# A gated linear recurrence and a SwiGLU block on one core: weights narrowed by integer operations on three engines, and another order of loads

## The chip, the cores and the metric

The kernel runs on one core of one Trainium2 chip. The metric is the device time of one execution in microseconds (us). The core has five engines with a queue of instructions each: TensorE (PE, with its weight loads shown as PEld), VectorE (DVE), ScalarE (ACT), GpSimd (POOL) and SyncE (SP), which here issues nearly all DMAs. An engine takes its instructions in program order; a wait in front of one holds all that stand behind it in the same queue.

## The reference, cut to what matters

```python
def _attn_ref(q, k, v, a_re, a_im):            # (4, 8, 768, 48) each
    mag = np.sqrt(a_re * a_re + a_im * a_im)
    scale = np.minimum(mag, 0.999) / (mag + 1e-06)
    a_re_n, a_im_n = (a_re * scale, a_im * scale)
    for t in range(S):
        new_re = ar * S_re - ai * S_im
        new_im = ar * S_im + ai * S_re
        kv = np.einsum('bhd,bhe->bhde', k[:, :, t], v[:, :, t])
        S_re, S_im = (new_re + kv, new_im)
        y[:, :, t] = np.einsum('bhd,bhde->bhe', q[:, :, t], S_re)

def _moe_ref(x, w_gate, w_val, w_out, rms_g):  # x: (3072, 384), d_ff 1536
    rms = np.sqrt(np.mean(x * x, axis=-1, keepdims=True) + 1e-06)
    xn = x / rms * rms_g
    g = xn @ w_gate
    silu = g * (1.0 / (1.0 + np.exp(-g)))
    val = xn @ w_val
    return (silu * val @ w_out).astype(np.float32)
```

The output of the first is laid out as 3072 rows of 384 and goes into the second. The three weight matrices arrive as float64, all other inputs as float32; the kernel computes in float32.

## The kernel before

The time axis is cut into 24 chunks of 128 steps (`C`), and two chunks make a unit (`UC`), so there are 12 units. A batch has three units. Within a chunk the recurrence is written as attention: k and q are turned by the running phase and scaled by the running magnitude of the gates, and a state of 96 x 48 per head carries from chunk to chunk. The work of the fast path (`fast`) lies in lanes, each a generator of steps:

- `load_gates` fetches a unit's gates `re` and `im` (L646, three DMAs each), `load_rows` its `k`, `q` (L662) and `v` (L669).
- `gates` (L683) works out phase and magnitude: about 13 ACT and 20 DVE operations on 128 x 768, in a chain that goes back and forth between the two, and ends with four products `ks`, `k`, `qs`, `q` (L768). `BEHIND` (L681) holds the first ACT step of units 2, 3 and 4 back until weight piece 9, 15 and 17.
- `move_rows` sends the four products to another partition layout, `kr` and `qr`, by three DMAs each (L782), then the decays of the chunks through DRAM and back (`dec` L792, `decay` L795). The second wait there is for a DMA that SP itself issued just before.
- `fetch` loads the float64 weights as pairs of 32-bit words in 18 pieces of 768 KB (L827), and `narrow` (L833) makes float32 of each: a piece has 128 x 768 numbers with a low and a high word. ACT squares the high word read as a float (L847); DVE masks out small values by that square (`masked`), shifts and joins the bits (L861 and the operation behind it), takes the power of two (L867), scales the low word by it and adds. Pieces 0 to 11 are `wg` and `wv` in turn, 12 to 17 are `wo`.
- `scores` runs s_ps = kr'qr (L888), the mask `am` on DVE (L893) and the transposes kt_ps (L907) with their copies `kt` on ACT (L911); `finish` runs state_ps (L928) and y_ps (L950, L953); `normalise` does the RMS norm with `rs` on POOL (L979) and the transposes xT_ps (L995, L1000).
- `feed_forward`, one lane for even and one for odd units, runs per unit 12 tiles gv_ps (L1023; 12 matmuls of 128 x 256 each), silu on ACT (L1027), `hT` on DVE (L587), then out_ps in halves (L1047), which need the `wo` pieces, a copy on ACT (L1056) and the store (L1059). gv_ps has three PSUM buffers.

The order of all instructions is fixed when the program is built. The class `Order` (L45) plays the lanes against each other: every step carries an engine, a planned duration and the names of the steps it waits for; of the steps at the heads of the lanes, the one that could begin first by this plan is written out next. On the chip an instruction waits only for the data and buffers it uses, but it stands in its engine's queue where the plan put it.

At the end a flag `bad` is worked out from range checks (`ok`, L1082). If it is set, a second, general program (`general`) runs after the fast one. With these inputs it isn't set.

Of the kernel before, what the change touches and what calls it, by code (L numbers as in the profile page):

```python
# [20 lines left out]
FP32 = mybir.dt.float32  # L21
I32 = mybir.dt.int32
U32 = mybir.dt.uint32
AF = mybir.ActivationFunctionType
ALU = mybir.AluOpType
# [3 lines left out]
P = 128  # L29
# [10 lines left out]
RE_MIN = 2.0 ** -7  # L40
RE_MAX = 2.0 ** 7
P_MIN = 2.0 ** -40


class Order:  # L45
# [72 lines left out]
def step(engine, us, needs, emit, **more):  # L118
    return engine, us, needs, emit, more
# [429 lines left out]
def fast(tc, ctx, qT, kT, v, a_re, a_im, w_gate, w_val, w_out, rms_g, out, H, bad):  # L549

    nc = tc.nc
    B, DM, S = a_re.shape
# [4 lines left out]
    DF = w_gate.shape[1]  # L557
    ND = DM // P
    NF = DF // P
    UC = 2  # L560
    T = UC * C
    NU = N // UC
# [11 lines left out]
    stage = ctx.enter_context(tc.tile_pool(name="stage", bufs=2))  # L574
    EARLY = 4
# [4 lines left out]
    order = Order()  # L580
    tt_us = lambda n: 0.07 + n / 960
    ts_us = lambda n: 0.07 + n / 1920
    ac_us = lambda n: 0.19 + n / 1200
    pe_us = lambda n: max(0.11, 0.003 + n / 1200)

    def tt(o, x, y, op=ALU.mult):
        nc.vector.tensor_tensor(out=o, in0=x, in1=y, op=op)  # L587

    def stt(o, x, c, y, op0, op1=ALU.mult, **kw):
        nc.vector.scalar_tensor_tensor(out=o, in0=x, scalar=c, in1=y, op0=op0, op1=op1, **kw)  # L590
# [32 lines left out]
    order.clock["POOL"] = 5.0  # L623
    ends = consts.tile([P, NU, ND, UC], FP32, name="ends")
    range_ = consts.tile([P, NU], FP32, name="range_")
    FW = 2 * P
    NW = DF // FW
    wg = consts.tile([P, NW, ND, FW], FP32, name="wg")
    wv = consts.tile([P, NW, ND, FW], FP32, name="wv")
    wo = consts.tile([P, NF, DM], FP32, name="wo")  # L630
# [6 lines left out]
    def load_gates():  # L637
        for u in range(NU):
            b, c = divmod(u * UC, NCH)
            t = UN[u]  # L640

            def gate(name, ap, queue, t=t, b=b, c=c):
                t[name] = prep.tile([P, ND, T], FP32, tag=name, name=name, bufs=2)
                rows = ap[b].rearrange("(h j l) s -> j l h s", j=ND, l=L)
                for j in range(ND):
                    queue.dma_start(out=t[name][:, j], in_=rows[j][:, :, c * C:c * C + T])  # L646

            for name, ap in (("re", a_re), ("im", a_im)):
                aside = u == 0 and name == "im"
                yield step("ACT" if aside else "SP", 0.0 if aside else 3 * order.ISSUE,  # L650
                           [("rot", u - 2) if u > 1 else None],
                           lambda name=name, ap=ap, q=nc.scalar if aside else nc.sync: gate(name, ap, q),
                           mb=0.39, ends=[(name, u)])

# [23 lines left out]

    BEHIND = {2: ("piece", 9), 3: ("piece", 15), 4: ("piece", 17)}  # L681

    def gates():  # L683
        n1 = ND * T
# [2 lines left out]
        for u in range(NU):  # L687
# [7 lines left out]

            yield E("ACT", ac_us(n1), [K("re"), ("rot", u - 1) if u else None, BEHIND.get(u)], begin, K("s0"))
            re, im, s, w, y, r, p, ks, qs = (t[x] for x in ("re", "im", "s", "w", "y", "r", "p", "ks", "qs"))
# [107 lines left out]
    parts = []  # L805
    for f in range(NW):
        parts += [(to[:, f], ap, slice(0, ND), f * FW) for to, ap in ((wg, w_gate), (wv, w_val))]
    parts += [(wo[:, c:c + 2], w_out, slice(c, c + 2), 0) for c in range(0, NF, 2)]
    raws = {}

    def fetch():

        def gains():
            nc.sync.dma_start(out=gcol, in_=rms_g.rearrange("(c p) -> p c", p=P))

        yield step("SP", 0.5, [], gains, mb=0.01, ends=["gains"])
        for i, (to, ap, c, f) in enumerate(parts):
            wide = ap.dtype != FP32

            def get(i=i, to=to, ap=ap, c=c, f=f, wide=wide):  # L820
                n = to.shape[2]
                if not wide:
                    nc.sync.dma_start(out=to, in_=ap.rearrange("(c p) f -> p c f", p=P)[:, c, f:f + n])
                    return
                pool = early if i < EARLY else stage
                raws[i] = pool.tile([P, to.shape[1], 2 * n], I32, tag="raw", name="raw")
                nc.sync.dma_start(out=raws[i], in_=ap.bitcast(I32).rearrange("(c p) f -> p c f", p=P)  # L827
                                  [:, c, 2 * f:2 * (f + n)])

            yield step("SP", 0.5, [("k", 0), ("piece", i - 2) if i >= EARLY + 2 else None], get,  # L830
                       mb=0.79 if wide else 0.39, ends=[("raw", i)])

    def narrow():  # L833

        for i, (to, ap, _, _) in enumerate(parts):
            if ap.dtype == FP32:
                yield step("NONE", 0.0, [("raw", i)], lambda: None, ends=[("piece", i)])
                continue
            n = to.shape[1] * to.shape[2]
            to = to.rearrange("p c f -> p (c f)")  # L840
            part = {}


            def square(i=i, to=to, part=part):
                words = raws.pop(i).rearrange("p c f -> p (c f)").rearrange("p (n two) -> p n two", two=2)
                part["lo"], part["hi"] = words[:, :, 0], words[:, :, 1]
                nc.scalar.activation(out=to, in_=part["hi"].bitcast(FP32), func=AF.Square)  # L847

            yield step("ACT", ac_us(n), [("raw", i)], square, ends=[("sq", i)])
            lo, hi = part["lo"], part["hi"]  # L850
            e, hf = to.bitcast(I32), hi.bitcast(FP32)
            ts = nc.vector.tensor_scalar

            def masked(to=to, hf=hf, part=part, n=n):
                stt(to, to, (1.125 * 2.0 ** -15) ** 2, hf, ALU.is_ge)
                part["t"] = stage.tile([P, n], I32, tag="t", name="t")

            yield step("DVE", tt_us(n), [("sq", i)], masked)
            t = part["t"]

            yield step("DVE", ts_us(n), [], lambda t=t, e=e: ts(  # L861
                out=t, in0=e, scalar1=3, scalar2=0x3FFFFFFF, op0=ALU.logical_shift_left,
                op1=ALU.bitwise_and))
            yield step("DVE", tt_us(n), [], lambda t=t, e=e: stt(t, e, -2 ** 30, t, ALU.bitwise_and,
                                                               ALU.bitwise_or))

            yield step("DVE", ts_us(n), [], lambda t=t, e=e: ts(  # L867
                out=e, in0=t, scalar1=-2 ** 23, scalar2=None, op0=ALU.bitwise_and))
            yield step("DVE", tt_us(n), [], lambda to=to, lo=lo: stt(to, lo.bitcast(U32), 2.0 ** -52, to,
                                                                   ALU.mult))  # L870
            yield step("DVE", tt_us(n), [], lambda to=to, t=t: tt(to, t.bitcast(FP32), to, ALU.add),
                       ends=[("piece", i)])


    order.free = {"a": [0.0] * 5, "g": [0.0] * 3}
# [132 lines left out]
    def feed_forward(groups):  # L1008
        for g in groups:
            t = UN[g]  # L1010
            for f in range(NF):

                def tile_(f=f, t=t):
# [5 lines left out]
                    t["gv", f] = ps = ps_g.tile([P, 2, T], FP32, tag="g", name="gv_ps")  # L1019
                    cols = slice(f * P % FW, f * P % FW + P)  # L1020
                    for i, w_ in enumerate((wg, wv)):
                        for d in range(ND):
                            nc.tensor.matmul(ps[:, i], lhsT=w_[:, f * P // FW, d, cols], rhs=t["xT"][:, d],  # L1023
                                             start=d == 0, stop=d == ND - 1)
# [49 lines left out]
    order.lane(gates(), 0.1)  # L1074
    order.lane(fetch(), 0.2)
    order.lane(narrow(), 0.3)
    with tc.manual_schedule():
        order.run()


    ne = NU * ND * UC
    ok = act.tile([P, DM], FP32, tag="xn", name="ok")[:, 0:2 * ne + NU]  # L1082
    for to, in_, limit, op in ((ok[:, 0:ne], ends.rearrange("p u j c -> p (u j c)"), P_MIN, ALU.is_ge),
                               (ok[:, ne:2 * ne], ends.rearrange("p u j c -> p (u j c)"), 1.0, ALU.is_le),
                               (ok[:, 2 * ne:], range_, 0.0, ALU.is_le)):
        nc.vector.tensor_scalar(out=to, in0=in_, scalar1=limit, scalar2=None, op0=op)
    okc = act.tile([P, 1], FP32, tag="okc", name="okc", bufs=1)
    nc.vector.tensor_reduce(out=okc, in_=ok, axis=mybir.AxisListType.X, op=ALU.add)
    ps = ps_a.tile([1, 1], FP32, tag="a", name="ok_ps")
    nc.tensor.matmul(ps, lhsT=okc, rhs=ones, start=True, stop=True)  # L1090
    nc.vector.tensor_scalar(out=bad, in0=ps, scalar1=-1.0, scalar2=float(P * (2 * ne + NU)),
                            op0=ALU.mult, op1=ALU.add)


# [47 lines left out]
```

## Time and profile before

| | us |
|---|---|
| median of 3 runs | 906.38 |
| lowest and highest run | 902.7, 909.99 |
| the profiled execution, its own time | 902.58 |
| span of its trace (first to last instruction) | 900.9 |
| mean granted TensorE clock in it | 0.916 |

The trace shows one execution. Rows of groups read: line, engine, operation, output and inputs, shapes, count, then busy time, mean ns of one, and the idle time just before them with the instruction that ended it. Rows of the timeline read: start, duration, engine, line, operation, count, and in brackets the idle time before it and what ended that. SPq is the queue of SP, whose rows are DMA issues. The granted clock is the share of full speed that TensorE was given.

Over the whole span the DMA queues moved 62.21 MB. The 18 narrowed pieces are 14.2 MB of that as read.

### The profile page before, as it was taken

Reading aid. Unit: us, or ns where it says so; the run is one execution under the profiler, and the core shown is the slowest. Engines: PE = TensorE matmul, PEld = TensorE weight load, DVE = VectorE, ACT = ScalarE, POOL = GpSimd, SP = SyncE. Lnnn points to the kernel's source line nnn. Section 1 sums busy time; section 2 is a strip of 40 time slices with the busy share of each in tenths; the row PEclk is TensorE's granted clock in tenths of the full one; section 3 lists DMA queues with packets and bytes.
Section 4 is the critical chain, followed back from the end, with each engine's and each line's share of the span. In section 5 each row is a group of like instructions: output and inputs, shape, how many; then the busy total and the mean of one; then the engine's idle time right before and its main releaser. Section 6 shows DMA issues by size and latency. Waiting matters only on the chain.

```text
span 900.9 us, 10071 instructions
## 1 busy us (share of the span) xinstructions
PE 790.7 (88%) x3946; PEld 654.2 (73%) x3946; DVE 443.0 (49%) x689; ACT 359.9 (40%) x566; POOL 18.9 (2%) x41
## 2 busy tenths in 40 slices
PE   0058889969279998999999999999999999999997
PEld 0057788858148797879886888878888867886684
DVE  5996468955967756566876765122111300111010
ACT  6625126613647664665867675120011201111010
POOL 0000000000000000000000000000000000000000
PEclk9975969965679999799999799999999989999999
DMA  8830752382075536547186470006000000000100
GB/s 271 159 95 12 107 161 92 71 173 90 0 123 117 112 43 116 81 96 106 53 129 126 93 111 1 1 13 95 18 1 0 1 17 18 1 1 0 36 1 21
DMA packets 70440, 62.21 MB, mean 69 GB/s; under 512 B 12016, under 2 KB 64240, under 8 KB 70384
## 3 DMA queue, kind: packets, MB, share of 16 engines
q1 hardware_dynamic: 69952, 61.08, 33.7%
q8 instruction: 33, 0.54, 0.3%
q10 hardware_dynamic: 432, 0.39, 0.2%
q14 instruction: 23, 0.19, 0.1%
HBM read 37.82 MB, written 4.76 MB: 47 GB/s over the span
## 4 chain that ended last, share of the span: by engine, by line
PE 74%; DVE 12%; DMA 5%; ACT 4%; issue 2%; SPq 2%; POOL 0%; DVEq 0%; ACTq 0%
PE gv_ps L1023 35%; PE out_ps L1047 19%; PE y_ps L950 6%; PE y_ps L953 5%; PE s_ps L888 3%; PE state_ps L928 3%; DMA dec<-ends 3%; PE kt_ps L907 1%; DVE t L590 1%; PE xT_ps L995 1%; SPq L782 1%; DVE wg L590 1%; DVE t L861 1%; DVE w L590 1%; SPq L646 1%
## 5 line engine op out<-in xcount | busy, mean ns | idle before, releaser
L1047 PE MATMUL out_ps<-wo,hT 128*128 128x384 f32 x576 | 204.9, 514 | 21.1 <-DVE wo L587 21.1
L1023 PE MATMUL gv_ps<-xT,wg 128*128 128x256 f32 x864 | 214.3, 385 | 1.7 <-DVE xT L1000 1.6
L1023 PE MATMUL gv_ps<-xT,wv 128*128 128x256 f32 x864 | 211.3, 381 | 0.0
L587 DVE TENSOR_TENSOR hT<-gv_ps,hT 128x256 f32<-128x256 f32 x144 | 60.2, 422 | 278.0 <-ACT hT L1027 277.4
L1047 PEld LDWEIGHTS out_ps<-wo,hT 128*128 128x128 f32 x576 | 114.6, 202 | 98.6 <-DVE wo L587 22.9
L1023 PEld LDWEIGHTS gv_ps<-xT,wg 128*128 128x128 f32 x864 | 164.3, 193 | 25.8 <-DVE xT L1000 2.0
L1023 PEld LDWEIGHTS gv_ps<-xT,wv 128*128 128x128 f32 x864 | 165.1, 191 | 22.8
L1027 ACT ACTIVATE hT<-gv_ps 128x256 f32<-128x256 f32 x144 | 54.9, 385 | 217.8 <-PE gv_ps L1023 217.4
L888 PE MATMUL s_ps<-qr,kr 96*128 96x128 f32 x384 | 55.7, 305 | 69.9 <-DMA dec<-ends 59.1
L888 PEld LDWEIGHTS s_ps<-qr,kr 96*128 96x128 f32 x384 | 52.5, 217 | 72.1 <-issue 65.1
L950 PE MATMUL y_ps<-v,am 128*128 128x48 f32 x384 | 81.4, 311 | 0.0
L953 PE MATMUL y_ps<-state,qr 96*128 96x48 f32 x320 | 73.4, 317 | 0.0
L950 PEld LDWEIGHTS y_ps<-v,am 128*128 128x128 f32 x384 | 69.4, 231 | 1.3 <-ACT kt L911 0.3
L953 PEld LDWEIGHTS y_ps<-state,qr 96*128 96x128 f32 x320 | 60.2, 234 | 0.0
L1056 ACT COPY ot<-out_ps 128x384 f32<-128x384 f32 x24 | 11.2, 479 | 105.9 <-PE out_ps L1047 104.5
L928 PEld LDWEIGHTS state_ps<-v,kt 128*96 128x96 f32 x320 | 35.7, 193 | 8.1 <-ACT kt L911 6.7
L928 PE MATMUL state_ps<-v,kt 128*96 128x48 f32 x320 | 36.0, 274 | 6.2 <-ACT kt L911 6.2
L893 DVE TENSOR_TENSOR am<-s_ps,causal 128x512 f32<-128x512 f32 x48 | 32.1, 686 | 16.1 <-PE s_ps L888 15.5
L911 ACT COPY kt<-kt_ps 128x384 f32<-128x384 f32 x40 | 17.8, 481 | 40.5 <-PE kt_ps L907 40.5
L979 POOL TENSOR_TENSOR rs<-ssq,mhalf 128x1 f32<-128x1 f32 x24 | 16.9, 703 | 795.5 <-DVE ssq L974 795.5
L970 ACT ACTIVATE xn<-y_ps 128x384 f32<-128x384 f32 x24 | 11.8, 490 | 46.0 <-PE y_ps L953 33.6
L1000 DVE TENSOR_TENSOR xT<-xT_ps,gcol 128x384 f32<-128x384 f32 x24 | 13.3, 556 | 34.0 <-PE xT_ps L995 30.1
(102 smaller groups left out, 710.6 us busy)
## 6 DMA issues: line engine op xcount, KB each, us to landing
re<-in_a_re_dram SPq DMA_DIRECT2D x36, 128.0 KB, 4.9
k<-in_k_dram SPq DMA_DIRECT2D x24, 192.0 KB, 3.6
q<-in_q_dram SPq DMA_DIRECT2D x24, 192.0 KB, 4.0
v<-in_v_dram SPq DMA_DIRECT2D x24, 192.0 KB, 4.0
raw<-in_w_gate_dram SPq DMA_DIRECT2D x6, 768.0 KB, 6.6
raw<-in_w_val_dram SPq DMA_DIRECT2D x6, 768.0 KB, 6.5
kr<-ks SPq DMA_DIRECT2D x36, 128.0 KB, 3.9
kr<-k SPq DMA_DIRECT2D x36, 128.0 KB, 5.1
```

The source lines that it names most:

```text
L587: nc.vector.tensor_tensor(out=o, in0=x, in1=y, op=op)
L590: nc.vector.scalar_tensor_tensor(out=o, in0=x, scalar=c, in1=y, op0=op0, op1=op1, **kw)
L888: nc.tensor.matmul(u["s_ps"][a][:, h], lhsT=u["k"][:, a * HH + h], rhs=u["q"][:, a * HH + h], start=True, stop=True)
L893: nc.vector.tensor_tensor(out=u["am"][a], in0=u["s_ps"][a], op=ALU.mult, in1=causal.unsqueeze(1).to_broadcast([C, HH, C]))
L911: nc.scalar.copy(out=u["kt"][a], in_=u["kt_ps"][a])
L928: nc.tensor.matmul(u["st_ps"][:, h], lhsT=u["kt"][h // HH][:, h % HH], rhs=u["v"][:, h], start=True, stop=True)
L950: nc.tensor.matmul(u["y_ps"][:, h], lhsT=u["am"][h // HH][:, h % HH], rhs=u["v"][:, h], start=True, stop=prev is None)
L953: nc.tensor.matmul(u["y_ps"][:, h], lhsT=u["q"][:, h], rhs=prev[:, h], start=False, stop=True)
L979: nc.gpsimd.tensor_tensor(out=u["rs"], in0=u["ssq"], in1=mhalf, op=ALU.pow)
L1023: nc.tensor.matmul(ps[:, i], lhsT=w_[:, f * P // FW, d, cols], rhs=t["xT"][:, d], start=d == 0, stop=d == ND - 1)
L1027: nc.scalar.activation(out=t["hT"][:, f], in_=t["gv", f][:, 0], func=AF.Silu)
L1047: nc.tensor.matmul(t["o_ps", i], lhsT=t["hT"][:, f, i * C:(i + 1) * C], rhs=wo[:, f], start=f == 0, stop=f == NF - 1)
```

## The change

The narrowing of a piece becomes four steps on three engines instead of seven on two:

- ACT reads the low word as an unsigned number and writes 2.0 + low x 2^-51, a float whose bits are 0x40000000 plus the rounded top bits of the low word (`share`).
- DVE shifts the high word left by 3 (`shifted`) and sets the sign bit of the high word into what ACT wrote (`signed`).
- POOL adds the two as 32-bit integers (`total`).

What was masked before (values too small for float32) is no longer looked at here. Instead a new lane, `small`, loads all 18 pieces a second time late in the program (the plan places them behind out_ps of unit 6 and later), takes the least absolute value of the high words per partition by a DVE reduction into `least_`, and the flag `bad` is set if one is below `HIGH_MIN`.

`BEHIND` is emptied. `load_gates` of a unit now waits in the plan for the last move of the rows two units before ("moved3") instead of for their products ("rot"), and the weight loads from the fifth on wait in the plan for the first unit's rows to have been moved.

```diff
+    least_ = consts.tile([P, 2 * (DF // (2 * P)) + NF // 2], FP32, name="least_")
+    nc.gpsimd.memset(least_, 1.0)
...
-                           [("rot", u - 2) if u > 1 else None],
+                           [("moved3", u - 2) if u > 1 else None],
...
-    BEHIND = {2: ("piece", 9), 3: ("piece", 15), 4: ("piece", 17)}
+    BEHIND = {}
+    CHECK = 6
...
-            yield step("SP", 0.5, [("k", 0), ("piece", i - 2) if i >= EARLY + 2 else None], get,
+            yield step("SP", 0.5, [("k", 0), ("piece", i - 2) if i >= EARLY + 2 else None,
+                                    ("moved3", 0) if i >= EARLY else None], get,
...
-                nc.scalar.activation(out=to, in_=part["hi"].bitcast(FP32), func=AF.Square)
...
-                stt(to, to, (1.125 * 2.0 ** -15) ** 2, hf, ALU.is_ge)
...
+            def share(i=i, to=to, part=part, n=n):
+                part["lo"], part["hi"] = words(raws.pop(i))
+                nc.scalar.activation(out=to, in_=part["lo"].bitcast(U32), func=AF.Copy, bias=2.0,
+                                     scale=2.0 ** -51)
                 part["t"] = stage.tile([P, n], I32, tag="t", name="t")
...
+            def shifted(part=part):
+                nc.vector.tensor_scalar(out=part["t"], in0=part["hi"], scalar1=3, scalar2=None,
+                                        op0=ALU.logical_shift_left)
+
+            def signed(to=to.bitcast(I32), part=part):
+                stt(to, part["hi"], -2 ** 31, to, ALU.bitwise_and, ALU.bitwise_or)
+
+            def total(to=to.bitcast(I32), part=part):
+                nc.gpsimd.tensor_tensor(out=to, in0=part["t"], in1=to, op=ALU.add)
+
+            yield step("ACT", 0.05 + ac_us(n), [("raw", i)], share, ends=[("share", i)])
+            yield step("DVE", tt_us(n), [("raw", i), ("piece", i - 2) if i > 1 else None], shifted)
+            yield step("DVE", tt_us(n), [("share", i)], signed, ends=[("both", i)])
+            yield step("POOL", 1.6, [("both", i)], total, ends=[("piece", i)])
+
+    def small():
...
+            def least(i=i):
+                nc.vector.tensor_reduce(out=least_[:, i:i + 1], in_=words(raws.pop(i))[1].bitcast(FP32),
+                                        axis=mybir.AxisListType.X, op=ALU.min, apply_absolute_value=True)
+
+            yield step("SP", 0.5, [("out", CHECK + i // 4), ("least", i - 2) if i > 1 else ("piece", len(parts) - 1)],
+                       get, mb=0.79, ends=[("again", i)])
+            yield step("DVE", tt_us(n), [("again", i)], least, ends=[("least", i)])
```

Since the order is planned from these steps, instructions also move that the diff doesn't name. On SP, from the last raw load ahead of the first unit's moves to that of the next unit's k, before:

```order
L827 DMA raw<-in_w_val_dram 128x3x512
L782 DMA kr<-ks 16x8x256 x3
L782 DMA kr<-k 16x8x256 x3
L646 DMA re<-in_a_re_dram 128x1x256 x3
L646 DMA im<-in_a_im_dram 128x1x256 x3
L782 DMA qr<-qs 16x8x256 x3
L782 DMA qr<-q 16x8x256 x3
L792 DMA dec<-ends 128x3x2
L795 DMA decay<-dec 48x16 x2
L662 DMA k<-in_k_dram 128x3x128 x2
```

And now, in the same place:

```order
L835 DMA raw<-in_w_val_dram 128x3x512
L786 DMA kr<-ks 16x8x256 x3
L786 DMA kr<-k 16x8x256 x3
L786 DMA qr<-qs 16x8x256 x3
L786 DMA qr<-q 16x8x256 x3
L796 DMA dec<-ends 128x3x2
L799 DMA decay<-dec 48x16 x2
L649 DMA re<-in_a_re_dram 128x1x256 x3
L649 DMA im<-in_a_im_dram 128x1x256 x3
L665 DMA k<-in_k_dram 128x3x128 x2
```

The loads of re and im went from the middle of the moves to behind decay, in every unit that has such loads; ahead of this place stand four raw loads instead of six.

On DVE, the rows up to the first mask `am` of unit 0, which stand among unit 1's gates, before:

```order
L861 TENSOR_SCALAR t<-wg 128x768
L590 SCALAR_TENSOR_TENSOR t<-wg,t 128x768
L867 TENSOR_SCALAR wg<-t 128x768
L590 SCALAR_TENSOR_TENSOR wg<-raw,wg 128x768
L587 TENSOR_TENSOR wg<-t,wg 128x768
L587 TENSOR_TENSOR im<-im,y 128x768
L587 TENSOR_TENSOR w<-s,r 128x768
L590 SCALAR_TENSOR_TENSOR s<-w,r 128x768
L587 TENSOR_TENSOR re<-re,y 128x768
L590 SCALAR_TENSOR_TENSOR w<-s,w 128x768
L893 TENSOR_TENSOR am<-s_ps,causal 128x512 x2
```

And now:

```order
L861 TENSOR_SCALAR t<-raw 128x768
L591 SCALAR_TENSOR_TENSOR wv<-raw,wv 128x768
L588 TENSOR_TENSOR im<-im,y 128x768
L588 TENSOR_TENSOR w<-s,r 128x768
L591 SCALAR_TENSOR_TENSOR s<-w,r 128x768
L588 TENSOR_TENSOR re<-re,y 128x768
L591 SCALAR_TENSOR_TENSOR w<-s,w 128x768
L591 SCALAR_TENSOR_TENSOR im<-re,im 128x768
L591 SCALAR_TENSOR_TENSOR w<-w,p 128x768
L915 TENSOR_TENSOR am<-s_ps,causal 128x512 x2
```

A piece takes two rows where it took six, and pieces 0 to 3 stand ahead of the mask instead of 0 to 4; two rows of the gates came ahead of it.

On PE, from the last xT_ps of unit 1 (its second chunk) on, the numbers of the buffers shown: before, 32 rows of gv_ps follow that transpose, and only then the first s_ps of unit 2, whose end of the stretch is

```order
L1023 MATMUL gv_ps_978<-xT_734,wg_115 128x256 x3
L1023 MATMUL gv_ps_978<-xT_734,wv_116 128x256 x3
L1023 MATMUL gv_ps_1001<-xT_734,wg_115 128x256 x3
L1023 MATMUL gv_ps_1001<-xT_734,wv_116 128x256 x3
L888 MATMUL s_ps_1039<-qr_996,kr_953 128x128 x4
L888 MATMUL s_ps_1044<-qr_996,kr_953 128x128 x4
L907 MATMUL kt_ps_1056<-ident_104,kr_953 128x96 x4
```

Now 8 rows of gv_ps stand between the transpose and unit 2's first s_ps:

```order
L1017 MATMUL xT_ps_773<-ident_104,xn_760 128x128 x3
L1045 MATMUL gv_ps_781<-xT_758,wg_117 128x256 x3
L1045 MATMUL gv_ps_781<-xT_758,wv_118 128x256 x3
L1045 MATMUL gv_ps_803<-xT_758,wg_117 128x256 x3
L1045 MATMUL gv_ps_803<-xT_758,wv_118 128x256 x3
L1045 MATMUL gv_ps_828<-xT_758,wg_117 128x256 x3
L1045 MATMUL gv_ps_828<-xT_758,wv_118 128x256 x3
L1045 MATMUL gv_ps_843<-xT_426,wg_117 128x256 x3
L1045 MATMUL gv_ps_843<-xT_426,wv_118 128x256 x3
L910 MATMUL s_ps_878<-qr_820,kr_791 128x128 x4
L910 MATMUL s_ps_883<-qr_820,kr_791 128x128 x4
```

So unit 2's attention stands 24 rows of gv_ps earlier, and the gv_ps rows follow later; units 3 to 5 came forward in the same way.

More of the change, by code (lines that the diff above doesn't have):

```diff
@@ L42 @@
 P_MIN = 2.0 ** -40
+HIGH_MIN = 1.125 * 2.0 ** -15
 class Order:
@@ L809, in fast, with words @@
     raws = {}
+    def words(raw):
+        two = raw.rearrange("p c f -> p (c f)").rearrange("p (n two) -> p n two", two=2)
+        return two[:, :, 0], two[:, :, 1]
     def fetch():
@@ L841, in narrow @@
             part = {}
[L844 to L851, printed above, removed]
@@ L852, in narrow @@
-            ts = nc.vector.tensor_scalar
-            def masked(to=to, hf=hf, part=part, n=n):
-                stt(to, to, (1.125 * 2.0 ** -15) ** 2, hf, ALU.is_ge)
-                part["t"] = stage.tile([P, n], I32, tag="t", name="t")
[L858 to L870, printed above, removed]
@@ L871, in narrow @@
-            yield step("DVE", tt_us(n), [], lambda to=to, t=t: tt(to, t.bitcast(FP32), to, ALU.add),
-                       ends=[("piece", i)])
+            def share(i=i, to=to, part=part, n=n):
+                part["lo"], part["hi"] = words(raws.pop(i))
+                nc.scalar.activation(out=to, in_=part["lo"].bitcast(U32), func=AF.Copy, bias=2.0,
+                                     scale=2.0 ** -51)
+                part["t"] = stage.tile([P, n], I32, tag="t", name="t")
+            def shifted(part=part):
+                nc.vector.tensor_scalar(out=part["t"], in0=part["hi"], scalar1=3, scalar2=None,
+                                        op0=ALU.logical_shift_left)
@@ new lines, in narrow, with get @@
+            yield step("POOL", 1.6, [("both", i)], total, ends=[("piece", i)])
+    def small():
+        for i, (to, ap, c, f) in enumerate(parts):
+            if ap.dtype == FP32:
+                continue
+            def get(i=i, to=to, ap=ap, c=c, f=f):
+                n = to.shape[2]
+                raws[i] = stage.tile([P, to.shape[1], 2 * n], I32, tag="raw", name="raw")
+                nc.sync.dma_start(out=raws[i], in_=ap.bitcast(I32).rearrange("(c p) f -> p c f", p=P)
+                                  [:, c, 2 * f:2 * (f + n)])
+            def least(i=i):
+                nc.vector.tensor_reduce(out=least_[:, i:i + 1], in_=words(raws.pop(i))[1].bitcast(FP32),
+                                        axis=mybir.AxisListType.X, op=ALU.min, apply_absolute_value=True)
+            n = to.shape[1] * to.shape[2]
+            yield step("SP", 0.5, [("out", CHECK + i // 4), ("least", i - 2) if i > 1 else ("piece", len(parts) - 1)],
+                       get, mb=0.79, ends=[("again", i)])
+            yield step("DVE", tt_us(n), [("again", i)], least, ends=[("least", i)])
@@ L1076, in fast @@
     order.lane(narrow(), 0.3)
+    order.lane(small(), 0.5)
     with tc.manual_schedule():
@@ L1081, in fast @@
     ne = NU * ND * UC
-    ok = act.tile([P, DM], FP32, tag="xn", name="ok")[:, 0:2 * ne + NU]
+    nl = least_.shape[1]
+    ok = act.tile([P, DM], FP32, tag="xn", name="ok")[:, 0:2 * ne + NU + nl]
     for to, in_, limit, op in ((ok[:, 0:ne], ends.rearrange("p u j c -> p (u j c)"), P_MIN, ALU.is_ge),
                                (ok[:, ne:2 * ne], ends.rearrange("p u j c -> p (u j c)"), 1.0, ALU.is_le),
-                               (ok[:, 2 * ne:], range_, 0.0, ALU.is_le)):
+                               (ok[:, 2 * ne:2 * ne + NU], range_, 0.0, ALU.is_le),
+                               (ok[:, 2 * ne + NU:], least_, HIGH_MIN, ALU.is_ge)):
         nc.vector.tensor_scalar(out=to, in0=in_, scalar1=limit, scalar2=None, op0=op)
@@ L1090, in fast @@
     nc.tensor.matmul(ps, lhsT=okc, rhs=ones, start=True, stop=True)
-    nc.vector.tensor_scalar(out=bad, in0=ps, scalar1=-1.0, scalar2=float(P * (2 * ne + NU)),
+    nc.vector.tensor_scalar(out=bad, in0=ps, scalar1=-1.0, scalar2=float(P * (2 * ne + NU + nl)),
                             op0=ALU.mult, op1=ALU.add)
```

## The prediction

> **What bounds the kernel now.** I read the page first, then the busy time by stretch, then TensorE's waits in order of time.
>
> ```profile
> span 900.9 us, 10071 instructions
> PE 790.7 (88%) x3946; PEld 654.2 (73%) x3946; DVE 443.0 (49%) x689; ACT 359.9 (40%) x566; POOL 18.9 (2%) x41
> ```
>
> ```profile
> 0.00:48.60 48.60, 0.00 (x0) 0.00 (x1) 37.70 (x48) 30.21 (x36) 2.04 (x17) 1.00 0.82 203
> 48.60:268.40 219.80, 171.43 (x771) 145.79 (x772) 158.32 (x228) 91.79 (x135) 4.43 (x6) 0.74 0.42 92
> 268.40:350.20 81.80, 76.25 (x487) 67.11 (x485) 53.74 (x82) 54.13 (x80) 2.28 (x3) 1.00 0.55 97
> 350.20:894.30 544.10, 543.00 (x2691) 441.34 (x2691) 193.11 (x331) 183.36 (x317) 10.15 (x15) 0.97 0.24 44
> ```
>
> Columns: the stretch and its length, then busy PE, PEld, DVE, ACT, POOL, the granted clock, DMA. After 350 us TensorE never stops, so the end lies as late as TensorE is late by then. By 350.2 it has lost 48.6 (nothing to do), 219.80 - 171.43 = 48.4 and 81.80 - 76.25 = 5.6 idle, and 171.43 x (1 - 0.74) = 44.6 to the low clock: 147 us. These four are what the change can touch. The last 544 us lose some 16 to the clock in either kernel.
>
> The idle time has these places (start, duration, idle before, releaser):
>
> ```profile
> 48.63 3.75 PE L888 MATMUL s_ps<-qr,kr 96*128 96x128 f32 x16 [48.63 <-DMA dec<-ends]
> ...
> 60.73 2.07 PE L888 MATMUL s_ps<-qr,kr 96*128 96x128 f32 x8 [6.14 <-DVE am L893]
> ...
> 82.61 0.90 PE L995 MATMUL xT_ps<-ident,xn 128*128 128x128 f32 x3 [2.64 <-ACT xn L982]
> 85.07 2.93 PE L1023 MATMUL gv_ps<-xT,wg 128*128 128x256 f32 x6 [1.56 <-DVE xT L1000]
> ...
> 105.88 2.02 PE L888 MATMUL s_ps<-qr,kr 96*128 96x128 f32 x16 [2.04 <-DMA qr<-q]
> ...
> 116.15 2.80 PE L928 MATMUL state_ps<-v,kt 128*96 128x48 f32 x16 [5.78 <-ACT kt L911]
> ...
> 191.18 3.75 PE L888 MATMUL s_ps<-qr,kr 96*128 96x128 f32 x16 [8.38 <-DMA dec<-ends]
> ...
> 238.71 2.93 PE L1047 MATMUL out_ps<-wo,hT 128*128 128x384 f32 x4 [10.31 <-DVE wo L587]
> 252.43 16.08 PE L1047 MATMUL out_ps<-wo,hT 128*128 128x384 f32 x40 [10.79 <-DVE wo L587]
> ```
>
> Everything before 268 us waits for rotated rows (s_ps) or narrowed weights (out_ps), and both come out of one DVE queue. The clock loss follows the waits: after one, attention matmuls run at half clock though TensorE is busy, until gv matmuls have run for some us:
>
> ```profile
> 70.00:75.00 5.00, 5.00 (x29) 5.00 (x29) 2.62 (x6) 4.70 (x7) 0.55 (x1) 0.50 0.01 2
> 95.00:100.00 5.00, 5.00 (x24) 4.38 (x24) 4.87 (x8) 0.77 (x2) 0.00 (x0) 1.00 1.13 205
> ```
>
> So a wait ahead of attention costs more than itself. (The Trainium skill, "TensorE: Matmul & The Clock Gate", Part 1, says that some 3.4 us of sustained activity lift the clock; the trace differs, 5.00 of 5.00 busy at 0.50. By the page the half-clock terms below would shrink to about 2 us a wait and the sum come out some 12 us lower.)
>
> **The change part by part.** Narrowing, per piece:
>
> ```profile
> L590 DVE SCALAR_TENSOR_TENSOR t<-wg,t 128x768 int32<-128x768 int32 x6 | 5.8, 958 | 0.2
> L861 DVE TENSOR_SCALAR t<-wg 128x768 int32<-128x768 int32 x6 | 3.4, 560 | 0.2
> L847 ACT ACTIVATE wg<-raw 128x768 f32<-128x768 f32 x6 | 5.4, 898 | 0.0
> ```
>
> Before, DVE runs four of the first kind and two of the second: 4 x 0.96 + 2 x 0.56 = 4.95 us, x18 = 89. Now it runs a shift of strided words (0.56 to 0.96; I take 0.9, since the input is strided) and one two-input operation (0.96): 1.86, x18 = 33. DVE is freed of 55 us, all before 250. ACT's share keeps its 0.90. POOL gets 18 integer adds, which no row shows. Nearest rows:
>
> ```profile
> L601 POOL MEMSET starts<- 128x768 f32 x1 | 0.7, 738 | 0.0
> L617 POOL TENSOR_SCALAR_AFFINE_SELECT causal<-causal 128x128 f32<-128x128 f32 x1 | 0.3, 290 | 0.0
> ```
>
> Written only, 768 columns take 0.74. Reading one input grows some 1.5 ns a column (290 ns at 128 less about 0.1 fixed), 1.25 for 768, and two inputs at most double: 0.74 to 2.4; I take 1.6, the middle. POOL has nothing else but rs. The shift of a piece waits for the add of the piece before last (t has two buffers), and behind the shift on DVE stand gates; an add has a whole piece's time for that, so I cost the wait at nothing unless an add passes 2.4 us. Whether DVE stands still meanwhile is open: 0 to 2.4 us an add; I take 1 us, near the middle, and both ends go into the range.
>
> Row order and loads. With re and im between the moves, from the first kr issue to the decay issue (which waits for dec to land) takes 107.34 - 87.65 = 19.7 us; unit 10, which has no loads left to slip in, takes 533.11 - 516.35 = 16.8:
>
> ```profile
> 87.65 1.85 SPq L782 DMA_DIRECT2D kr<-ks  x3
> ...
> 107.34 2.74 SPq L795 DMA_DIRECT2D decay<-dec  x2
> 110.13 0.43 SPq L827 DMA_DIRECT2D raw<-in_w_val_dram  x1
> ```
> ```profile
> 516.35 1.85 SPq L782 DMA_DIRECT2D kr<-ks  x3
> ...
> 533.11 0.80 SPq L795 DMA_DIRECT2D decay<-dec  x2
> ```
>
> So each unit's rows land 2.9 us sooner: kr issue to s_ps was 105.88 - 87.65 = 18.2 and becomes 15.6 at most. re and im of the unit after next now stand behind decay, but are wanted a whole unit later: nothing. Weights queued behind decay, though, keep their wait: raw issues at 110.13, a load lands 4.4 to 6.6 us later, and ACT, which takes its steps in order, stands on it ahead of kt and arctan.
>
> ```profile
> raw<-in_w_gate_dram SPq DMA_DIRECT2D x6, 768.0 KB, 6.6
> ...
> raw<-in_w_out_dram SPq DMA_DIRECT2D x6, 768.0 KB, 4.4
> ```
>
> The 12 move DMAs of a unit are now one run on SP, and two of the first six raw loads come after them: those are narrowed after unit 0's ks anyway.
>
> Now TensorE's work. Matmuls at full clock:
>
> ```profile
> 519.75 62.16 PE gv_ps L1023 x288
> ...
> 600.15 1.72 PE y_ps L950 x16
> ...
> 878.71 15.49 PE out_ps L1047 x48
> ```
>
> These are 0.216, 0.108 and 0.323 us each (s_ps, state and transposes near y's). Counted down the PE order, full-clock work ahead of the first s_ps of units 1 to 5 was 29, 91, 127, 159, 202 us and is now 29, 60, 92, 126, 155; the first out_ps stands at 88 instead of 104. The order asks for rows every 32 us, where before there were 62 to spare at unit 2. So the term that decides is how fast the gates now come. Before:
>
> ```profile
> 29.95 1.93 SPq L782 DMA_DIRECT2D kr<-ks  x3
> ...
> 247.62 1.84 SPq L782 DMA_DIRECT2D kr<-ks  x3
> ...
> 283.66 1.85 SPq L782 DMA_DIRECT2D kr<-ks  x3
> ```
>
> With some five pieces between, units 0 and 1 lie 57.7 apart (to 87.65); with narrowing all but done, 283.66 - 247.62 = 36.0. Now, per unit: DVE rows from one ks to the next come to 32 to 35 us, plus 3.5 adds x 1 us, plus about 4 us where ACT stands on a raw load queued behind decay: 40 on average.
>
> Place by place:
> - Start. kr(0) leaves about 0.5 earlier (two DVE operations fewer ahead of it, one add beside it) and lands 2.9 sooner: 48.6 becomes 45.3.
> - The wait for am (6.1) goes: DVE is there at about 47, PE wants it at 51. PE then runs at half clock as before (busy some 33 us up to 91 at 0.50, so 16.6 us of loss) with both normalise waits (4.2). s_ps of unit 1: 45.3 + 29 + 16.6 + 4.2 = 95; its rows, kr at 76.7 and 15.6 after, are there, so the 2.0 go.
> - kt waits for the raw load behind decay: 5.8 becomes 1.6.
> - kr of units 2 to 5: 121, 163, 203, 236; rows 15.6 later: 137, 179, 219, 251.
> - PE is at unit 2 by 128: it waits 9 (8.4 before), and the attention behind loses 5 to the clock. The first out_ps wants piece 14 at about 175: 4.7 (21.1 before), and 3 of clock. Units 4 and 5: 2.8 and 2.3, clock 1.
> - Second read: 18 loads and reduces (0.56 to 0.96) in the last 544 us, where DVE is busy 193 and DMA at 0.24: nothing, while a hT tile waits less than the two spare PSUM tiles of 2.6 us. The loads stand among the stores on SP, which have the same slack; their last block is over before the last two stores.
>
> Sum: 45.3 + idle (4.2 + 1.6 + 9 + 4.7 + 2.8 + 2.3 = 24.6) + clock (16.6 + 9 = 25.6) = 95.5 against 147.2: 51.7 less. The profiled execution's own time, 902.58, gives 851; the median of runs, 906.38, is 0.4% above it. I say 853.
>
> **The rivals**, by the mean distance c between kr issues of units 1 to 5: each us of c costs four, since TensorE stands behind (853 at c = 40).
> - DVE stands for the whole of every add: 14 adds x 2.4 = 34 us in four units instead of 14, c = 45: 873, and up to 880 with half clock behind the longer waits. For it: DVE is back to back there. (The Trainium skill, "SBUF — State Buffer", Who interferes with whom, says just this: a GpSimd operation that reads SBUF and a DVE operation with two SBUF inputs shut each other out for a whole instruction. No run here shows it yet. "GPSIMD Engine Reference", 3.1, has 4497 ns for 2048 columns, so an estimate of 1.7 us an add, and by it 18 x 1.7 = 31 us given back on DVE.)
> - The gates keep TensorE fed (c at 36 or below, as at 247.62): waits of units 2 to 5 and their clock go, 825 to 835. Against it: 3.5 pieces still lie in each unit.
> - Gates gain nothing: c near 53. Then lateness at unit 5 equals today's, and the time is 897 to 915. It would take adds that also hold the pieces back.
> - Slower: the new order moved gv work behind attention, so if the gates come at the pace of units 0 and 1 (c = 57.7), TensorE is late by 4 x 17.7 = 71 more than I say: 924. It decides from c = 53. Against it: the 24 us of narrowing in those 57.7 shrink to 9.
>
> **How the numbers follow.** c between 36 and 44 (835 to 868): 0.66; DVE held by adds (868 to 893): 0.15; fed (below 835): 0.08; no change: 0.05; slower: 0.06. A measurement of this kernel tells about 1% (897 to 915) from no change. Faster 0.89, same 0.05, slower 0.06. The range, 832 to 880, holds the first, half of the third and most of the second.
>
> **What would show it.** Right: PE starting near 45, no wait at am, out_ps waiting under 6 us for wo, kr issues of units 1 to 5 about 40 apart, clock above 0.8 over the first 250 us, reduces at the end without a PE wait. Wrong: adds over 2.4 us, DVE's two-input operations longer than 0.96 beside them, c over 50, or hT waiting for least.

## The result and the profile after

| | before | after |
|---|---|---|
| median of 4 runs, us | 904.54 | 873.08 |
| lowest and highest run | 901.74, 909.99 | 868.18, 879.88 |
| profiled execution: own time, span | 902.58, 900.9 | 879.88, 878.2 |

The ratio is 0.965, 95% interval 0.9555 to 0.9746: faster by 3.5%, and 20 us above the 853 forecast. The profiled execution is the slowest of the four. In four of the experiments below (the new order alone, `BEHIND` emptied, rows first, high words only) one or two runs lie over 1.5% above the kernel's fastest; the medians given are over all runs, and without those they would be 928, 858, 869 and 824 us.

The span, the busy times and the busy time by stretch of the changed kernel (columns as in the prediction's table):

```profile
span 878.2 us, 10090 instructions
...
PE 794.1 (90%) x3946; PEld 659.4 (75%) x3946; DVE 419.6 (48%) x636; ACT 358.9 (41%) x566; POOL 58.9 (7%) x60
```
```profile
45.00:250.00 205.00, 175.80 (x894) 156.57 (x895) 151.09 (x210) 120.56 (x174) 37.30 (x22) 0.85 0.61 130
250.00:350.00 100.00, 97.08 (x508) 81.62 (x507) 64.54 (x94) 67.02 (x94) 1.26 (x1) 0.91 0.61 102
```

TensorE's waits over the whole span, as totals (us, times, longest):

```profile
PE s_ps L910 <- DMA dec<-ends: 50.0, 2, 45.4
PE state_ps L950 <- ACT kt L933: 10.3, 3, 4.6
PE s_ps L910 <- DMA qr<-q: 8.7, 2, 6.0
PE xT_ps L1017 <- ACT xn L1004: 4.8, 3, 3.5
PE gv_ps L1045 <- DVE xT L1022: 3.2, 2, 2.1
```

The waits for narrowed weights (21.1 us before) and for am (6.1) are gone, and the start is at 45.4 for 48.6. What is left are mainly the start, waits for rows (13.2 us besides the start) and a larger total for kt (10.3 us for 6.2 before).

One ledger serves for all kernels below: how late TensorE is at 350 us, that is 350 less the full-clock durations of the matmuls begun by then (0.216 us for gv, 0.323 out, 0.108 y and xT, 0.115 s, 0.082 state and kt). The time in which it isn't busy is "idle" (the start included), the rest is "slow": matmuls that ran at less than full clock. Rounded to us, each from its one profiled execution:

| kernel | idle | slow | late at 350 | span |
|---|---|---|---|---|
| before | 102 | 45 | 148 | 900.9 |
| after | 77 | 53 | 130 | 878.2 |
| predicted for after | 70 | 26 | 96 | |

Span less lateness is 753 and 749: past 350 us little changed. The forecast's idle time was 7 us too low and its clock loss 27 too low. The slow time goes by the durations of the matmuls and not by the granted clock, for here the two differ: between 45 and 75 us the clock of the changed kernel reads 1.00, while 16 matmuls of s_ps take 3.75 and 3.67 us, for 1.95 at 95.29.

### The profile page after: what moved, and what is told of

It is laid out like the page before. It is cut to its first block, busy times and chain, and to the rows that moved or that the text cites. A ratio compares the mean times of both kernels' runs of the same rounds, so it can differ in the third digit from the quotient of the medians.

```text
span 878.2 us, 10090 instructions
## 1 busy us (share of the span) xinstructions
PE 794.1 (90%) x3946; PEld 659.4 (75%) x3946; DVE 419.6 (48%) x636; ACT 358.9 (41%) x566; POOL 58.9 (7%) x60
## 4 chain that ended last, share of the span: by engine, by line
PE 78%; DMA 10%; DVE 4%; ACT 3%; issue 2%; SPq 2%; POOL 0%; DVEq 0%; ACTq 0%
PE gv_ps L1045 36%; PE out_ps L1069 21%; PE y_ps L972 6%; DMA dec<-ends 5%; PE s_ps L910 5%; PE y_ps L975 5%; PE state_ps L950 4%; DMA kr<-k 2%; PE kt_ps L929 2%; DMA raw<-in_w_val_dram 1%; SPq L786 1%; DMA qr<-q 1%; PE xT_ps L1017 1%; DVE ks L588 1%; DMA raw<-in_w_out_dram 1%
## 5 line engine op out<-in xcount | busy, mean ns | idle before, releaser
L1045 PE MATMUL gv_ps<-xT,wg 128*128 128x256 f32 x864 | 220.8, 393 | 3.9 <-DVE xT L1022 3.2
L1045 PE MATMUL gv_ps<-xT,wv 128*128 128x256 f32 x864 | 214.2, 385 | 0.0
L1069 PE MATMUL out_ps<-wo,hT 128*128 128x384 f32 x576 | 198.7, 502 | 0.0
L1045 PEld LDWEIGHTS gv_ps<-xT,wg 128*128 128x128 f32 x864 | 168.0, 197 | 29.9 <-issue 2.5
L1045 PEld LDWEIGHTS gv_ps<-xT,wv 128*128 128x128 f32 x864 | 167.7, 194 | 24.0
L1069 PEld LDWEIGHTS out_ps<-wo,hT 128*128 128x128 f32 x576 | 112.2, 198 | 72.9 <-issue 7.0
L950 PE MATMUL state_ps<-v,kt 128*96 128x48 f32 x320 | 36.1, 274 | 10.3 <-ACT kt L933 10.3
L888 DVE TENSOR_REDUCE least__115<-raw 128x1 f32<-128x768 f32 x18 | 17.0, 945 | 46.7 <-DMA raw<-in_w_gate_dram 28.7
```

Of the source, the lines that this page charges most:

```text
L950: nc.tensor.matmul(u["st_ps"][:, h], lhsT=u["kt"][h // HH][:, h % HH], rhs=u["v"][:, h], start=True, stop=True)
L1069: nc.tensor.matmul(t["o_ps", i], lhsT=t["hT"][:, f, i * C:(i + 1) * C], rhs=wo[:, f], start=f == 0, stop=f == NF - 1)
```

## The experiments

Two theories at first. A: the adds hold DVE, and that lengthens c (45.8 measured, 40 predicted). B: DVE stands for TensorE and ACT, and the adds only fill what would be idle anyway. The runs soon brought another question, what the order rules do. Theory O says that TensorE's new order asks for rows too early, theory L that the new place of loads and moves on SP is what costs. Every run was timed against the kernel before on the same chip (medians 903.2 to 905.6); of each the median, then the ratio's interval.

**Without the adds.**

```
-                nc.gpsimd.tensor_tensor(out=to, in0=part["t"], in1=to, op=ALU.add)
+                pass
```


> The changed kernel without its 18 integer adds on POOL (their places in the order stay; the weights then lack the shifted high word, so the output is another). Theory A, the adds hold DVE: the 13 adds between the kr issues of units 1 and 5 stretch DVE's operations by about 1.5 us each, some 18 us; without them c falls from 45.8 to about 41 and the time from 873 to about 855. Theory B, DVE stands idle in that stretch for results of TensorE and ACT (42 us in the four units) and the adds only fill part of what would be idle anyway: c stays above 44 and the time above 866. Either way the two-input operations, the scan p and the copy turn should all come back to their short times (0.96, 1.76 and 0.17 us).

856.0 us (0.9392 to 0.9537): 17 less than with them, as A said. But c falls only to (238.92 - 66.74) / 4 = 43.0, between the two theories. That brings the kr issue of unit 5 forward by 11 us; another 10 come from the distance between units 0 and 1. DVE's groups in the stretch of units 1 to 5, with the adds and, in the second fence, without:

```profile
L732 DVE TENSOR_TENSOR_SCAN p<-w,starts 128x768 f32<-128x768 f32 x4 | 8.5, 2132 | 0.1
L588 DVE TENSOR_TENSOR k<-k,r 128x768 f32<-128x768 f32 x4 | 6.8, 1705 | 0.1
...
L756 DVE COPY turn<-im 128x3 f32<-128x3 f32 x4 | 3.7, 916 | 0.1
```
```profile
L732 DVE TENSOR_TENSOR_SCAN p<-w,starts 128x768 f32<-128x768 f32 x4 | 7.0, 1757 | 0.1
L588 DVE TENSOR_TENSOR k<-k,r 128x768 f32<-128x768 f32 x4 | 3.8, 958 | 0.1
...
L756 DVE COPY turn<-im 128x3 f32<-128x3 f32 x4 | 0.7, 169 | 0.1
```

Taken over all such groups up to the kr issue of unit 5, DVE's operations are 22.0 us longer with the 18 adds: 1.2 us an add.

**The two halves of the change apart.** First the new narrowing in the old order:

```
-                           [("moved3", u - 2) if u > 1 else None],
+                           [("rot", u - 2) if u > 1 else None],
...
-    BEHIND = {}
+    BEHIND = {2: ("piece", 9), 3: ("piece", 15), 4: ("piece", 17)}
...
-                                    ("moved3", 0) if i >= EARLY else None], get,
```


> The new narrowing and the second read with the order rules of before (re and im as soon as rot is done, weight loads from piece 4 not behind the moves of unit 0, gates of units 2 to 4 behind pieces 9, 15 and 17). By the terms of the prediction most of the gain comes from the shorter narrowing: start back at about 48.5 and rows some 3 us later per unit, time about 880 to 890. Rival, the order carries the gain: 895 to 905.

850.6 us (0.9312 to 0.9475), 22 less than the changed kernel and better than either guess. Then the same three rules the other way, put into the kernel before:

> The kernel before with the new order rules alone (re and im behind the moves, loads behind the moves of unit 0, gates behind no piece); its narrowing stays on DVE and no word is read twice. By the terms of the prediction the order gives 3 us at the start and 3 us a unit on the way to the rows, but c stays near 50 or more, since the 89 us of narrowing stay on DVE: 895 to 905. Rival, the order carries the gain: 880 to 890.

936.6 us (1.0277 to 1.0468): the new order alone makes the kernel 24 to 32 us slower, outside both guesses. Its start is at 45, and decay is issued 16.4 to 16.9 us after kr, as the prediction has it for that rule; but TensorE now waits longer for narrowed weights, which no rule puts ahead of the gates any more. TensorE's waits there:

```profile
PE s_ps L889 <- DMA dec<-ends: 56.3, 2, 45.0
PE out_ps L1048 <- DVE wo L587: 30.1, 2, 20.9
PE gv_ps L1024 <- DVE wv L587: 20.9, 2, 18.9
```

So all of the gain is the narrowing's (-54), and the order takes 22 of it back.

**Without the second read.** The lane `small` is left out:

```
-    order.lane(small(), 0.5)
```


> The changed kernel without the second read of the raw words (small values are then not looked for). The prediction priced the read at nothing: 873 within 4. Rival, the 18 loads and reduces cost something in the last 520 us, or their waits reach TensorE: 868 or less.

874.2 us (0.9564 to 0.97): the read costs nothing that can be told.

**Each order rule put back alone.** In the changed kernel BEHIND, re and im, and the loads of pieces 4 and 5 get their old rule, one at a time, with the lines of the diff above:

> The changed kernel with one order rule put back: the gates of units 2 to 4 stand behind pieces 9, 15 and 17 again. Full-clock work ahead of the first s_ps of units 1 to 5 in TensorE's order becomes 29, 84, 134, 161, 199 us, where the changed kernel has 29, 60, 92, 126, 155. Theory O, TensorE's order asks for rows too early: the waits of units 2, 4 and 5 for rows (6.0, 4.5, 2.7 us) and the half clock behind them go, 848 to 858. Theory L, what costs is that raw loads stand behind the moves and decay: that stays, 866 to 876.

> The changed kernel with one order rule put back: re and im of the unit after next leave as soon as rot is done, so between the moves. TensorE's order then has 29, 67, 101, 133, 167 us ahead of the rows of units 1 to 5, and rows land some 3 us later. Theory O: the 7 to 12 us more outweigh the 3, 860 to 868. By the terms of the prediction alone (rows 2.9 us later for each unit, start at 48): 876 to 886.

> The changed kernel with one order rule put back: the loads of pieces 4 and 5 leave at 13 to 15 us, ahead of unit 0's moves, not behind them. TensorE's order then has 29, 69, 99, 127, 168 us ahead of the rows of units 1 to 5. Theory O: a gain of some 8 us as with the early re and im, 860 to 868; the start stays near 45. Theory L: ACT no longer stands 6 us on raw loads ahead of kt in units 1 and 2, and most of the 22 us between the two orders comes back, 850 to 858.

868.3 (0.9582 to 0.9685), 877.3 (0.9672 to 0.9725) and 870.1 us (0.9581 to 0.9692), against 873.1: none gives back much. From the other side, one new rule in the old order:

> The run with the old order (850.6) with one new rule: the gates of units 2 to 4 stand behind no piece. Full-clock work ahead of the rows of units 1 to 5 falls from 34, 76, 130, 163, 204 to 31, 71, 104, 140, 179. Theory O: TensorE comes some 25 us of work sooner to the rows of units 3 to 5 and waits again, 862 to 870. If the gates come as much sooner: 845 to 854.

> The run with the old order (850.6) with one new rule: re and im of the unit after next leave behind the moves, so the rows land some 3 us sooner and the start is 45 for 48.6. By the terms of the prediction (3.3 at the start and 2.9 a unit) 842 to 848. Theory O: the plan answers with less work ahead of the rows (26, 67, 112, 145, 184 for 34, 76, 130, 163, 204), which takes it back: 852 to 866.

858.2 (0.9403 to 0.9513), between its two guesses, and 869.8 us (0.9532 to 0.9652). The seven orders side by side, all with the new narrowing:

| re, im behind moves | loads behind moves | BEHIND empty | us |
|---|---|---|---|
| no | no | no | 850.6 |
| no | no | yes | 858.2 |
| yes | no | no | 869.8 |
| yes | no | yes | 870.1 |
| no | yes | yes | 877.3 |
| yes | yes | no | 868.3 |
| yes | yes | yes (the change) | 873.1 |

With either rule that sends rows ahead of loads the time is 868 or more, with both no worse than with one. The clearest miss is that of the run with re and im alone behind the moves (869.8), which the prediction's terms put at 842 to 848: rows came 3 us sooner after kr (17.0, 16.7, 17.0 for 20.0, 20.0, 19.6) and the start 3 us sooner, and the time was 19 us longer. The gates came later: kr of unit 1 at 81.52 for 75.49, of unit 2 at 139.93 for 130.27. Theory O had its sign, though it put the time below what came.

**SP's wait between the decay's two transfers.** In the old order, one step of the plan becomes two, so that SP issues other DMAs while the write of ends lands:

```
-            yield step("SP", 1.3, [("p", u)], decays, mb=0.02, then=2.5, ends=[("rows", u)])
+            yield step("SP", 0.6, [("p", u)], written, mb=0.01, then=5.0, ends=[("dec", u)])
+            yield step("SP", 0.7, [("dec", u)], decays, mb=0.01, then=0.5, ends=[("rows", u)])
```


> The new narrowing in the order of before, with the two transfers of the decay apart in SP's order: first the write of ends, then loads of weights and of the next rows, then decay when the write has landed. If SP's stand on the write (some 9 us a unit, with raw loads queued behind it, and ACT on them ahead of kt) is on the path, the waits for kt go (5.1 us) and the gates come closer together: 838 to 846. If it is covered by other work, or if loads now ahead of decay hold the rows back, 848 to 856.

855.9 us (0.941 to 0.9489): no gain. Loads now slip in between the moves too (decay is issued 22 to 25 us after kr), and the waits for kt grow:

```profile
PE s_ps L912 <- ACT kt L935: 11.1, 1, 11.1
```

**Feed-forward work put ahead of attention by hand.**

```
+    FILL = {4: [("gv", 1, 3)], 6: [("up", 1), ("out", 0)], 8: [("gv", 2, 4)], 10: [("up", 2), ("out", 1)]}
...
-            yield step("PE", 2 * H * pe_us(C), rows, pairs, then=0.2, ends=[("s", n)], takes=("a", 2))
+            yield step("PE", 2 * H * pe_us(C), rows + FILL.get(n, []), pairs, then=0.2, ends=[("s", n)], takes=("a", 2))
```


> The changed kernel with one thing more: the attention of units 2 to 5 is planned only after a stretch of feed-forward work (gv of group 1 up to its fourth; gv of group 1 and the outputs of group 0; gv of group 2 up to its fifth; gv of group 2 and the outputs of group 1). The order rules for rows, loads and gates stay the new ones. Full-clock work ahead of the first s_ps of units 1 to 5 becomes 29, 65, 131, 164, 210 us, near the 34, 76, 130, 163, 204 of the run with the old order. Theory O, TensorE's order asks for rows too early and it stands, then runs attention at half clock, with feed-forward work behind it: 850 to 860. Theory L, the place of the loads and moves on SP is what costs: 868 to 880.

868.5 us (0.9481 to 0.9641): at the lower edge of theory L's range, outside theory O's, and not told apart from the changed kernel. The waits for rows are gone but for the start; in their place TensorE waits for hT, whose DVE step frees a PSUM tile and stands in DVE's queue among the gates:

```profile
PE s_ps L911 <- DMA dec<-ends: 45.0, 1, 45.0
PE gv_ps L1046 <- DVE hT L588: 14.3, 3, 8.2
PE state_ps L951 <- ACT kt L934: 4.4, 1, 4.4
```

So theory O in its simple form, that TensorE's order alone is at fault, falls.

**Only the high words, in the old order.** The share on ACT and the add on POOL go; DVE does two operations a piece:

```
+                nc.vector.tensor_scalar(out=part["t"], in0=part["hi"], scalar1=3, scalar2=0x3FFFFFFF,
+                                        op0=ALU.logical_shift_left, op1=ALU.bitwise_and)
...
+                stt(to, part["hi"], -2 ** 30, part["t"], ALU.bitwise_and, ALU.bitwise_or)
```


> The new narrowing in the order of before (850.6), and of it only the high words: two DVE operations a piece (shift and mask, then the sign), no share on ACT, no add on POOL. It leaves out the rounding by the low words: the weights are cut, not rounded. If the adds and the share still set the pace there as in the changed kernel (17 us without the adds): 830 to 842. If TensorE waits for little in that order anyway (12 us between 75 and 350): 845 to 852.

831.1 us (0.9124 to 0.9262), 20 to 27 less than with the adds and the share in that order. The weights are cut here, not rounded, as the low words are left out. The stretches again:

```profile
45.00:250.00 205.00, 195.55 (x1146) 168.54 (x1146) 144.54 (x227) 127.90 (x189) 9.23 (x9) 0.94 0.60 127
250.00:350.00 100.00, 98.82 (x556) 85.28 (x556) 68.00 (x103) 67.90 (x93) 1.74 (x2) 0.95 0.65 107
```

There is no wait for kt left in it. The ledger of these kernels (the profile of the high words is of their fastest run):

| kernel | idle | slow | late at 350 | span | c |
|---|---|---|---|---|---|
| high words, old order | 56 | 20 | 76 | 819.6 | 44.4 |
| old order | 67 | 28 | 95 | 846.3 | 49.7 |
| no adds | 68 | 36 | 104 | 851.2 | 43.0 |
| feed-forward ahead | 73 | 46 | 119 | 865.2 | 44.4 |
| the change | 77 | 53 | 130 | 878.2 | 45.8 |
| before, new order | 128 | 51 | 178 | 924.6 | 43.0 |

Span less lateness is 744 to 753 in all of them: lateness at 350 sets the time, and c does not.

## Why the prediction was right in sign and short in size

The 873 measured lies in the range, 832 to 880, near its slow end. (The last step of its sum, 851 raised by 0.4%, gives 854 and not 853.) Of the signs named beforehand the start, am, wo and the reduces came out as "right" has them, and the clock by its record (0.85 from 45 to 250 us; by the durations of the matmuls some 0.75); c did not (45.8 for 40), and two signs of "wrong" came: adds over 2.4 us (6 of 18) and two-input operations of DVE longer than 0.96 beside them.

- **The start, am, wo, the second read.** The start is at 45.42 (45.3 forecast), am isn't waited for, wo not at all (4.7 forecast), the reduces take 0.945 each and the run without them shows no cost. These steps held.
- **Narrowing.** The shift takes 0.55 alone and 0.81 on average (0.9 taken), an add 1.81 alone and 2.13 on average (1.6 taken). DVE is held for 1.2 us an add, not the 1 taken and far from the 2.4 of the first rival; without them the time falls 17, where the forecast charged 14 and that rival 34. So the rival's 873, met to the us, is not its mechanism's doing alone. An add and an operation of DVE that begins just behind it:

```profile
73.86 2.29 POOL L868 TENSOR_TENSOR wg<-t,wg 128x768 int32<-128x768 int32 x1
```
```profile
73.51 0.96 DVE L588 TENSOR_TENSOR k<-k,r 128x768 f32<-128x768 f32 x1
74.39 2.58 DVE L588 TENSOR_TENSOR q<-q,p 128x768 f32<-128x768 f32 x1
```

  The add begins while the first DVE operation runs and takes 2.29 for 1.81; the second of DVE's takes 2.58 for 0.95, as it gets on only when the add ends. The trace agrees with the rule of the Trainium skill's "SBUF — State Buffer" (Who interferes with whom) that the prediction set against its 1 us; but not every add found such an operation behind it (no DVE operation ran beside the one at 88.84), so the average was 1.2 us an add.
- **The step that failed: "each us of c costs four, since TensorE stands behind".** The last table refutes it: c of 49.7 with 846.3, of 43.0 with 924.6. TensorE has feed-forward work to do while rows are late, if its order has it there.
- **The term that was mis-sized: kt and the clock behind it.** The prediction gave the wait for kt 1.6 us and no clock. It is 10.3: the attention of units 1 and 3 breaks on it (4.6 and 4.2 us), that of units 2, 4 and 5 on rows, and each time the matmuls behind run at half clock (behind the third wait for kt, 1.60 us in unit 2, they don't). ACT and then TensorE in unit 1, and state_ps at full clock later, then in unit 3:

```profile
102.99 0.89 ACT L856 ACTIVATE wv<-raw 128x768 f32<-128x768 uint32 x1 [6.29 <-DMA raw<-in_w_val_dram]
103.78 0.85 ACT L933 COPY kt<-kt_ps 128x384 f32<-128x384 f32 x2
```
```profile
97.74 1.98 PE L910 MATMUL s_ps<-qr,kr 96*128 96x128 f32 x16
104.30 2.79 PE L950 MATMUL state_ps<-v,kt 128*96 128x48 f32 x16 [4.58 <-ACT kt L933]
...
114.94 2.76 PE L950 MATMUL state_ps<-v,kt 128*96 128x48 f32 x16
117.50 2.89 PE L1045 MATMUL gv_ps<-xT,wg 128*128 128x256 f32 x6
...
160.73 1.56 PE L950 MATMUL state_ps<-v,kt 128*96 128x48 f32 x16 [1.60 <-ACT kt L933]
...
203.52 2.79 PE L950 MATMUL state_ps<-v,kt 128*96 128x48 f32 x16 [4.16 <-ACT kt L933]
```

  At 97.74 the matmuls go at full clock; behind the 4.58 us at half, 2.79 us for 16 that take 1.56 at 160.73. By stretches, the slow time is 15 us up to 83 (16.6 forecast; 6 with BEHIND put back, so in part chance), 9 and 6 behind the two longer waits for kt (104 to 123, 203 to 215), 8 behind the three waits for rows (6 forecast), and 10 in two spells with no gap just ahead of them (166 to 176, 296 to 308), which no term of the prediction covers and no run explains. The waits for rows themselves were near: 6.0 at unit 2 (9 forecast), 4.5 and 2.7 at units 4 and 5 (2.8 and 2.3). That ACT stands on a raw load behind decay was in the prediction as 4 us of gate time; that kt stands behind such a load again in units 2 and 3, and attention's clock with it, was not priced. The run that takes the share off ACT has no wait for kt and 20 us of slow time for 53 (past 90 us, 14 for 37), which fits; as it takes away the adds too and has the old order, it doesn't isolate the share. The run meant to free SP moved the wait instead.
- **The order.** It was booked as a gain of 3 us at the start and 2.9 a unit; both are seen, and as a whole it costs 22. The fourth rival named this (gv work moved behind attention) and asked 924 of it.

**What stays open.** Which wait makes the old order better than the new one isn't isolated. What the traces show: TensorE stands 13.2 us for rows besides the start and 10.3 for kt with the change, 2.3 and 5.1 in the old order, whose start is 3.2 us later. Between 45 and 262 us DVE stands 16.0 us for state_ps with the change and 2.9 in the old order (but 10.8 and 41.9 for hT), and ACT stands 19.6 (13.2 + 6.4) and 9.8 us (5.2 + 4.6) for raw loads. DVE's rows, first the change, then the old order:

```profile
DVE state L588 <- PE state_ps L950: 16.0, 7, 5.3
```
```profile
DVE state L588 <- PE state_ps L949: 2.9, 3, 1.3
```

Each rule changes the planned order on every engine, so one rule alone tells only about the order that came of it. An order of the old rules with loads alone behind the moves wasn't run.

## What to carry to other kernels

Work that a planner orders anew should be tried with its old order too: here the arithmetic alone is 22 us better than the arithmetic with the order that came with it. Price a wait inside a chain of small matmuls at its length plus, where it is long (over 4 us for kt here, not 1.6), the half clock behind it, and look for it where an engine that takes its steps in order has a load ahead of that chain's copy. A transfer that lands 3 us sooner can cost more than it gains when what feeds the next one comes later, as in the run with re and im alone behind the moves.

## What the runs showed of the hardware

- The same first matmuls, begun at the same time, ran at another clock in two kernels whose TensorE order agrees there. The changed kernel, then the one with BEHIND put back:

```profile
45.42 3.75 PE L910 MATMUL s_ps<-qr,kr 96*128 96x128 f32 x16 [45.42 <-DMA dec<-ends]
...
57.49 3.54 PE L972 MATMUL y_ps<-v,am 128*128 128x48 f32 x16
```
```profile
45.40 3.75 PE L910 MATMUL s_ps<-qr,kr 96*128 96x128 f32 x16 [45.40 <-DMA dec<-ends]
...
53.73 1.91 PE L972 MATMUL y_ps<-v,am 128*128 128x48 f32 x16
```

  In the second the matmuls went to full clock some 4.2 us after the start (at 49.6, within a row of kt_ps), and fell back to half at about 60 amid matmuls without a gap; in the first they stayed at half until 82, the first 25 us of it without a gap. The Trainium skill, "TensorE: Matmul & The Clock Gate", Part 1, puts the rise around 4 us into sustained activity; the second trace agrees, the first doesn't. By 75 us that is 13 us of slow time against 6. The runs of the changed kernel spread from 868 to 880, so single profiles here are not told apart below some 10 us; why the clock rose in one and not in the other is open.
- A copy of 128 x 3 on DVE took 1.66 us beside an add for 0.17 without: a small operation can be held for 1.5 us too.
